# Attention and a mixture of experts in one kernel: an expert's last second layer put between the chains of its tiles

## The chip, the cores and the metric

The kernel runs on one core of a Trainium2 chip. Five engines work from queues of their own: PE (TensorE, matmuls and transposes), DVE (VectorE), ACT (ScalarE), POOL (GpSimd) and SP, which here only starts transfers. They wait for each other by semaphores. The metric is the device time in microseconds; below 0.2% of it, about 1 us, two kernels can't be told apart here.

## The reference, cut to what matters

```python
scores = scale * np.matmul(q, k.transpose(0, 1, 3, 2))     # 4 x 8 heads, 576 x 64, fp32
scores = np.where(block_i >= block_j, scores, -1000000000.0)
attn_out = np.matmul(softmax(scores), v)
x = attn_out.transpose(0, 2, 1, 3).reshape(2304, 512)
logits = x @ w_gate                                        # 8 experts
expert_idx = np.argmax(logits, axis=1)
# each token goes to one expert, the first 576 tokens of an expert are kept
h = np.maximum(np.einsum('ecd,edf->ecf', disp, w1), 0.0)   # 512 -> 1024
y = np.einsum('ecf,efd->ecd', h, w2)                       # 1024 -> 512
out[i] = gate_w[i] * y[expert_idx[i], pos[i]]
```

How many tokens each expert gets is known only while the kernel runs.

## The kernel before, in words

Until about 231 us the kernel computes the attention, writes its rows to DRAM and sorts tokens into lists, one list for each expert. The change leaves this part alone but for three small operations. The rest is the expert stage.

**Slots and tiles.** The expert stage walks through nine slots, z = 0 to 8. Slot 0 is expert 0 with the tokens that were known early, slot 1 the rest of expert 0, and slots 2 to 8 are the other experts that have tokens at all. A slot has 1 to 5 tiles of 128 tokens. In this run the slots 0 to 6 have 3, 3, 1, 1, 5, 1 and 4 tiles, 18 in all, and slots 7 and 8 are empty.

**A tile.** `xin` transposes the tile's x on PE (4 transposes), ACT casts the result to `xh`, and DVE subtracts to get the rest `xl`. `l1(z, t, f)` is one half of the first layer: 12 matmuls of 128x512, each product being three (high by high, high by low, low by high), followed by ACT's relu into `hr[f]`. `htr` transposes `hr` on PE, ACT casts `hh`, and DVE subtracts `hl`. `l2` is the second layer, 24 matmuls in all, and `l2_out` scales the result on DVE (`yo`) and scatters it from POOL. `hh` and `hl` stand in one buffer each, so that the second layer of one tile must be through before the next tile's `htr` ends.

**Software pipeline.** `chain(z, t)` runs the first layer of tile t, then the second layer of the tile *before* it, then the transposes of h of tile t. For t = 0 the tile before is the last tile of the slot before, whichever that was. At t = 0 the chain also prepares the x of the next slot's first tile, `xin(z + 1, 0)`.

**Chains and branches.** `more(z, t, cnt)` puts each further tile into an `If` that is nested in the one before. `rest(z)` puts each further slot into an `If` with an `Else` that holds the last second layer. Every engine takes its own branch. Where the remaining tiles aren't there, each engine runs a short block that waits until it has finished its own work, raises its semaphores by what the skipped tiles would have raised, and jumps to the join. Work after the join can wait only for these raised counts. The counts of tiles are loaded into registers of all engines (`cnt`, L911), before slot 1.

**Weights.** Each expert's weights are 8 chunks of 512 KB, which pass through a ring of 8 buffers in the order of `STREAM`. `prep` of a chunk is an ACT cast to `whi`, a DVE subtraction to `wlo`, and the start of the load that comes next in the ring. `splits(z)` merges 8 of them evenly with the units of `chain(z, 0)`.

Of the kernel before, what the change touches and what calls it, by code (L numbers as in the profile page):

```python
# [39 lines left out]
FIRST_TILE = "RRRFRRRRFRRRFRHRHHR"  # L40
# [11 lines left out]
def attn_moe_kernel(  # L52
# [11 lines left out]
    nc = tc.nc  # L64
# [115 lines left out]
    on_i = const.tile([1, NZ, CT - 1], I32, name="on_i")  # L180
    idf = const.tile([P, E, FR, 2], F32, name="idf")
# [10 lines left out]
    def init_consts():  # L192
# [8 lines left out]
        nc.gpsimd.tensor_scalar_add(eid, iota8[0:1], float(E))  # L201
        nc.vector.tensor_tensor(
# [200 lines left out]
    def c_counts():  # L403
# [25 lines left out]
        has_more(ctl[:, 0, :], 1, NZ)  # L429

# [319 lines left out]
    HC = KF // 4 * 2  # L750
# [64 lines left out]
    def second(ws):  # L815
        return [lambda f=f: l2(ws, f, f + KF // 4) for f in range(0, KF, KF // 4)] + [l2_out]
# [8 lines left out]
    def first(z, t):  # L825
        us = [lambda: l1(z, t, 0), lambda: l1(z, t, 1), lambda: xin(z, t + 1)]
# [30 lines left out]
    def splits(z):  # L857
        if z == 1:
            return preps(G0, G0 + KD)
        g = G0 + KD + NCH * (z - 2)  # L860
        return preps(g, g + NCH)

    def tile_units(z, t):
# [3 lines left out]
    def chain(z, t, cnt):  # L867
# [92 lines left out]
```

## Time and profile before

| | |
|---|---|
| device time, median of 3 runs | 509.03 us (508.82 to 509.41) |
| the profiled execution, its own time | 505.01 us |
| its span in the trace | 503.3 us |
| PE busy | 456.6 us, 91% of the span |
| DVE, ACT, POOL busy | 278.0, 261.0, 117.9 us |
| mean granted PE clock | 0.977 of full speed |

The profiled execution is 1.71 us longer than its span, and 4.02 us shorter than the median of the timed runs. In the rows further down a number in square brackets is the time for which an engine stood idle just before, with what released it. L881 is the line of `more`'s `If`, so that a release by "ACTq L881" comes from ACT's branch block and not from an arithmetic instruction.

### The profile page before, as it was taken

How to read it: one execution, taken by the hardware profiler on the slowest of the kernel's cores; microseconds unless marked ns; L12 is line 12 of the kernel's file. 1: busy time of each engine (PE TensorE's matmuls, PEld its weight loads, DVE VectorE, ACT ScalarE, POOL GpSimd, SP SyncE). 2: the span in 40 equal slices, each digit the busy share in tenths (PEclk: the TensorE clock that was granted, in tenths of full speed). 3: DMA queues.
4: the chain of work that ended last, by engine and by line, in shares of the span. 5: the costliest groups of instructions: out<-in, count | busy, mean ns of one | idle time of the engine just before them, and what ended most of it. 6: DMA issues, size and time to landing. Idle time of an engine off the chain costs nothing. (4 is left out here: it accounts for less than half of the span.)

```text
span 503.3 us, 8359 instructions
## 1 busy us (share of the span) xinstructions
PE 456.6 (91%) x2786; PEld 365.1 (73%) x2786; DVE 278.0 (55%) x566; ACT 261.0 (52%) x613; POOL 117.9 (23%) x166
## 2 busy tenths in 40 slices
PE   5999999999999999989896999688999999899961
PEld 4777777777777777866675778566888888678851
DVE  7666677965696777944722332287662226772210
ACT  4877777777865976762222332268542217652200
POOL 6000001241113200131341411314242114252110
PEclk9999999999999999999999999889899999999977
DMA  4633656668463331112275320077991004992000
GB/s 113 147 77 72 188 145 192 157 125 232 142 192 92 84 70 46 43 34 78 83 224 210 117 85 22 21 264 238 315 317 55 22 21 152 307 308 102 21 29 17
DMA packets 87964, 64.90 MB, mean 129 GB/s; under 512 B 69866, under 2 KB 69866, under 8 KB 87904
## 3 DMA queue, kind: packets, MB, share of 16 engines
q1 hardware_dynamic: 83392, 55.26, 37.5%
q0 software_dynamic: 4512, 8.89, 5.4%
q8 instruction: 31, 0.51, 0.4%
q14 instruction: 29, 0.24, 0.2%
HBM read 53.54 MB, written 14.22 MB: 135 GB/s over the span
## 5 line engine op out<-in xcount | busy, mean ns | idle before, releaser
L589 ACT ACTIVATE p<-s,nm 128x512 f32<-128x512 f32 (+5 forms) x126 | 62.7, 501 | 36.7 <-DVE nm L588 33.1
L780 PE MATMUL h<-whi,xh 128*128 128x512 f32 x144 | 59.7, 415 | 11.9 <-ACTq L881 6.4
L784 ACT ACTIVATE hr<-h 128x512 f32<-128x512 f32 x36 | 21.5, 598 | 85.4 <-PE h L780 76.7
L588 DVE TENSOR_REDUCE nm<-s 128x1 f32<-128x512 f32 (+5 forms) x126 | 54.5, 450 | 19.3 <-PE s L582 14.0
L582 PE MATMUL s<-kh,bdh 128*128 128x192 f32 (+6 forms) x158 | 56.9, 360 | 5.9 <-ACT p L589 3.5
L803 PE MATMUL y<-whi,hh 128*128 128x512 f32 x144 | 58.6, 407 | 4.0 <-issue 4.0
L780 PE MATMUL h<-whi,xl 128*128 128x512 f32 x144 | 58.2, 404 | 0.0
L780 PE MATMUL h<-wlo,xh 128*128 128x512 f32 x144 | 58.1, 403 | 0.0
L803 PE MATMUL y<-whi,hl 128*128 128x512 f32 x144 | 57.2, 397 | 0.0
L803 PE MATMUL y<-wlo,hh 128*128 128x512 f32 x144 | 57.0, 396 | 0.0
L615 PE MATMUL w<-ident,p 128*128 128x128 f32 x400 | 54.7, 274 | 0.7 <-DVE bdl L547 0.6
L792 ACT CAST hh<-t 128x512 fp32r<-128x512 f32 x36 | 20.2, 594 | 59.3 <-issue 36.8
L641 PE MATMUL xB<-pt,vn 128*64 128x320 f32 (+2 forms) x320 | 49.2, 384 | 1.5 <-ACT pt L625 1.5
L582 PE MATMUL s<-kl,bdh 128*128 128x192 f32 (+6 forms) x158 | 50.0, 316 | 0.0
L582 PE MATMUL s<-kh,bdl 128*128 128x192 f32 (+6 forms) x158 | 49.6, 314 | 0.0
L809 DVE TENSOR_SCALAR yo<-y,itl 128x512 f32<-128x512 f32 x18 | 13.5, 749 | 64.3 <-PE y L803 60.0
L246 POOL DMA_INDIRECT xt<-x_rows,it x32 | 40.3, 1260 | 30.9 <-issue 10.4
L615 PEld LDWEIGHTS w<-ident,p 128*128 128x128 f32 x400 | 44.1, 141 | 4.7 <-issue 3.6
L149 POOL TENSOR_TENSOR wlo<-stg,whi 128x1024 fp32r<-128x1024 f32 x8 | 19.0, 2370 | 114.9 <-ACT whi L148 114.9
L149 DVE TENSOR_TENSOR wlo<-ring,whi 128x1024 fp32r<-128x1024 f32 x29 | 35.0, 1220 | 19.3 <-ACT whi L148 19.3
L769 DVE TENSOR_TENSOR xl<-t,xh 128x512 fp32r<-128x512 f32 x25 | 16.8, 688 | 50.7 <-ACT xh L768 50.7
L780 PEld LDWEIGHTS h<-whi,xh 128*128 128x128 f32 x144 | 28.2, 196 | 19.6 <-ACTq L881 7.1
(162 smaller groups left out, 861.2 us busy)
## 6 DMA issues: line engine op xcount, KB each, us to landing
ring<-in_moe_w_dram SPq DMA_DIRECT2D x34, 512.0 KB
stg<-in_moe_w_dram SPq DMA_DIRECT2D x26, 512.0 KB
out_dram<-xt SPq DMA_DIRECT2D x6, 768.0 KB
vn<-in_v_dram SPq DMA_DIRECT2D x32, 128.0 KB
x_rows<-xr SPq DMA_DIRECT2D x16, 256.0 KB
qn<-in_q_dram SPq DMA_DIRECT2D x30, 128.0 KB
kn<-in_k_dram SPq DMA_DIRECT2D x30, 128.0 KB
qn<-in_q_dram SPq DMA_DIRECT2D x16, 32.0 KB
```

Source lines behind the costliest of these rows:

```text
L149: tc.keep_in_program_order((nc.gpsimd if s == 0 else nc.vector).tensor_sub(lo, t, hi.bitcast(F32)))
L246: nc.gpsimd.indirect_dma_start(out=xt(z, t)[0:r], out_offset=None, in_=xd[0:rows], in_offset=bass.IndirectOffsetOnAxis(ap=it[z % NIT][0:r, ...
L582: nc.tensor.matmul(ps[:, 0:w], qs[i][:, b].rearrange("p j q -> p (j q)"), ks[:, a:a + w], start=(x == 0), stop=(x == 2),)
L588: nc.vector.tensor_reduce(nm[:, b:b + 1], pss[0][:, 0:n], axis=AX.X, op=ALU.max, negate=True)
L589: nc.scalar.activation(p_sb[i][b][:, 0:n], pss[0][:, 0:n], AF.Exp, bias=nm[:, b:b + 1], accum_out=sums[bi % 2][:, b % 2, hp, b // 2:b // 2 ...
L615: nc.tensor.transpose(ps[:, o:o + P], p_sb[i][b][:, t * P:(t + 1) * P], ident)
L641: nc.tensor.matmul(xp[j * D:(j + 1) * D, (b0 - r0) * BLK:(b0 - r0 + nb) * BLK], vn[:, t, j, :], pv[:, :, j, :], start=first and n_ == 0, s ...
L769: nc.vector.tensor_sub(xl, pv, xh.bitcast(F32))
L780: nc.tensor.matmul(ps, x_[:, kc], w_[:, fs], start=(kc == 0 and x == 0), stop=(kc == KD - 1 and x == 2))
L784: nc.scalar.activation(hr[f], ps, AF.Relu)
L792: nc.scalar.copy(hh[:, sl], pv)
L803: nc.tensor.matmul(ycur[0], h_[:, fc], w_, start=(fc == 0 and x == 0), stop=(fc == KF - 1 and x == 2))
```

## The change

The last second layer of a slot leaves `chain(z + 1, 0)` and stands in a function of its own, `tail(z)`, behind the join of the slot's branches and ahead of the next slot's branch; `rest` needs no `Else` then. `htr` and `l2` go by three pieces of h, (0,4), (4,6) and (6,8). For t of 1 and more they alternate: a piece of `l2` of the tile before, then the transposes of the same piece. For t = 0, with no second layer inside, the order is `l1`, `l1`, first piece of `htr`, `xin(z, 1)`, `xin(z + 1, 0)`, second and third piece. The eight splits part into four of the first layer, among the first six units of `chain(z, 0)`, and four of the second layer, in `tail(z)`. Each slot's count is loaded at the end of its `chain(z, 0)` instead of eight in a row, and `slot_i` tells PE ahead of time which way a slot's branch will go. PSUM is dealt out anew: `ps_h` 3 to 2 banks, `ps_y` 2 to 1, `ps_t` 3 to 5. Both gathers of slot 0 are issued before its first tile, and the first tile's units are interleaved with the routing in another order.

```diff
-FIRST_TILE = "RRRFRRRRFRRRFRHRHHR"
+FIRST_TILE = "RRRTTRRRRTRRRTRRTTTTR"
...
-    STREAM += [(1, c) for c in range(KD)]
-    for s in range(1, E):
-        if s + 1 < E:
-            STREAM += [(s + 1, c) for c in range(KD)]
-        STREAM += [(s, c) for c in range(KD, NCH)]
+    STREAM += [(s, c) for s in range(1, E) for c in range(NCH)]
...
-    ps_h = ctx.enter_context(tc.tile_pool(name="ps_h", bufs=3, space=PSUM))
-    ps_y = ctx.enter_context(tc.tile_pool(name="ps_y", bufs=2, space=PSUM))
-    ps_t = ctx.enter_context(tc.tile_pool(name="ps_t", bufs=3, space=PSUM))
+    ps_h = ctx.enter_context(tc.tile_pool(name="ps_h", bufs=2, space=PSUM))
+    ps_y = ctx.enter_context(tc.tile_pool(name="ps_y", bufs=1, space=PSUM))
+    ps_t = ctx.enter_context(tc.tile_pool(name="ps_t", bufs=5, space=PSUM))
...
+    PIECES = [(0, 4), (4, 6), (6, 8)]
...
-    def htr(f):
+    def htr(f0, f1):
         ps = ps_t.tile([P, 512], F32, tag="t", name="t")
-        pv = ps.rearrange("p (k n) -> p k n", n=P)
-        for x in range(4):
-            nc.tensor.transpose(pv[:, x, :], hr[f][:, x * P:(x + 1) * P], ident)
-        sl = slice(4 * f, 4 * f + 4)
-        nc.scalar.copy(hh[:, sl], pv)
-        nc.vector.tensor_sub(hl[:, sl], pv, hh[:, sl].bitcast(F32))
+        pv = ps.rearrange("p (k n) -> p k n", n=P)[:, 0:f1 - f0]
+        for fc in range(f0, f1):
+            nc.tensor.transpose(pv[:, fc - f0, :], hr[fc // 4][:, fc % 4 * P:(fc % 4 + 1) * P], ident)
+        nc.scalar.copy(hh[:, f0:f1], pv)
+        nc.vector.tensor_sub(hl[:, f0:f1], pv, hh[:, f0:f1].bitcast(F32))
...
+    def tile_units(z, t):
+        us = [lambda: l1(z, t, 0)]
+        if t + 1 < CT:
+            us.append(lambda: tell(z, t))
+        us += [lambda: l1(z, t, 1), lambda: xin(z, t + 1)]
         if t == 0:
+            us.insert(-1, lambda: htr(*PIECES[0]))
             us.append(lambda: xin(z + 1, 0))
-        return us
-
-    def turn(z, t):
-        return [lambda: keep_ids(z, t), lambda: htr(0), lambda: htr(1)]
+        for x, f in enumerate(PIECES):
+            if t:
+                us.append(lambda f=f: l2(ws_of(z), *f))
+            if t and x == len(PIECES) - 1:
+                us.append(l2_out)
+            if t or x:
+                us.append(lambda f=f: htr(*f))
+        return us + [lambda: keep_ids(z, t)]
...
-        if t + 1 < CT:
-            tell(z, t)
-        if t + 2 < CT:
+        if t + 2 < CT and (z, t) != (0, 1):
             gather(z, t + 2, ROWS0 if z == 0 else N)
         if t == 0:
             fetch(z)
-        for u in merge(tile_units(z, t), splits(z) if t == 0 else []):
+        us = tile_units(z, t)
+        for u in merge(us[:6], splits(z, 0)) + us[6:] if t == 0 else us:
             u()
-        more(z, t + 1, cnt)
+        more(z, t + 1, cnt if t else count(z))
+
+
+    def tail(z):
+        tc.no_sync_barrier()
+        if 0 < z < NZ - 1:
+            on = nc.values_load(
+                slot_i[0:1, z:z + 1], engines=[mybir.EngineType.PE], min_val=0, max_val=1,
+                skip_runtime_bounds_check_because="a comparison")
+            tc.mark_branch_hint_location(f"slot{z}", hint=on, engines=[mybir.EngineType.PE])
+        for u in merge(second(ws_of(z)), splits(z, 1)):
+            u()
...
     def rest(z):
-        if z == NZ:
-            for u in second(ws_of(z - 1)):
-                u()
-            return
-        with tc.If(cnt[z - 1] > 0, preferred_fallthrough_block=True) as some:
-            chain(z, 0, cnt[z - 1])
-            rest(z + 1)
-        with some.Else():
-            for u in second(ws_of(z - 1)):
-                u()
+        if z < NZ:
+            with tc.If(active > z - 1, preferred_fallthrough_block=True, label=f"slot{z - 1}"):
+                chain(z, 0)
+                tail(z)
+                rest(z + 1)
```

How the instructions stand now is shown at three places. Here is PE at the end of slot 1 in the kernel before: the branch block of the skipped tiles (L881, the block waits for PE's own count), the register loads, the branch of `rest`, and the first layer of slot 2.

```order
L881 UNCONDITIONAL_BRANCH
L881 UNCONDITIONAL_BRANCH [waits PE_49]
L881 UNCONDITIONAL_BRANCH [waits PE_49,PE_sequencer_49] x3
L911 TENSOR_LOAD ctl_i x7
L925 COMPARE_AND_BRANCH
L835 TENSOR_LOAD on_i
L956 BRANCH_PREFETCH_HINT
L780 MATMUL h<-whi_3111,xh_3127 128x512 [waits Activation_49]
L780 MATMUL h<-wlo_3112,xh_3127 128x512
L780 MATMUL h<-whi_3111,xl_3128 128x512 [waits DVE_49]
```

The first matmul behind the join waits for the count that ACT raises in its branch block, and the third one for DVE's.

The same place of the changed kernel, on PE, down to the end of the tail's second layer (L807 is the matmul of `l2`, L947 the branch of `rest`, L785 the matmul of `l1`).

```order
L903 UNCONDITIONAL_BRANCH
L903 UNCONDITIONAL_BRANCH [waits PE_49]
L903 UNCONDITIONAL_BRANCH [waits PE_49,PE_sequencer_49] x3
L934 TENSOR_LOAD slot_i
L894 TENSOR_LOAD slot_i
L976 BRANCH_PREFETCH_HINT
L807 MATMUL y<-whi_72,hh 128x512 [waits DVE_49,Activation_49]
L807 MATMUL y<-wlo_73,hh 128x512
L807 MATMUL y<-whi_72,hl 128x512
```

The first matmul behind the join is now one of `l2`, and it waits for the counts of both ACT and DVE; seven register loads have left, two have come. At the end of the same tail stands:

```order
L807 MATMUL y<-whi_78,hl 128x512 [waits DVE_49]
L807 MATMUL y<-whi_78,hh 128x512
L807 MATMUL y<-wlo_79,hh 128x512
L807 MATMUL y<-whi_78,hl 128x512
L947 COMPARE_AND_BRANCH
L785 MATMUL h<-whi_3114,xh_3130 128x512
L785 MATMUL h<-wlo_3115,xh_3130 128x512
L785 MATMUL h<-whi_3114,xl_3131 128x512
```

The next slot's first layer follows the tail with no wait of its own.

The third place is DVE in the first tile of slot 2. Before, from behind the join (`wlo` are the splits, `yo` and `hl` the work of `l2_out` and `htr`):

```order
L149 TENSOR_TENSOR wlo_65<-ring_3371,whi_64 128x1024
L149 TENSOR_TENSOR wlo_67<-stg_61,whi_66 128x1024
L769 TENSOR_TENSOR xl_3132<-t,xh_3131 128x512
L769 TENSOR_TENSOR xl_3130<-t,xh_3129 128x512
L149 TENSOR_TENSOR wlo_69<-stg_62,whi_68 128x1024
L149 TENSOR_TENSOR wlo_71<-stg_63,whi_70 128x1024
L149 TENSOR_TENSOR wlo_3120<-ring_3367,whi_3119 128x1024
L149 TENSOR_TENSOR wlo_3122<-ring_3368,whi_3121 128x1024
L809 TENSOR_SCALAR yo<-y,itl 128x512
L149 TENSOR_TENSOR wlo_3124<-ring_3369,whi_3123 128x1024
L793 TENSOR_TENSOR hl<-t,hh 128x512
L149 TENSOR_TENSOR wlo_3126<-ring_3370,whi_3125 128x1024
```

The changed kernel, a slot's first tile on DVE, down to its branch (L144 the splits, L797 `hl`, L774 `xl`, the first of them for the slot's own next tile and the second for the next slot):

```order
L144 TENSOR_TENSOR wlo_3115<-ring_3380,whi_3114 128x1024
L144 TENSOR_TENSOR wlo_3117<-ring_3381,whi_3116 128x1024
L797 TENSOR_TENSOR hl<-t,hh 128x512
L144 TENSOR_TENSOR wlo_3119<-ring_3382,whi_3118 128x1024
L774 TENSOR_TENSOR xl_3135<-t,xh_3134 128x512
L144 TENSOR_TENSOR wlo_3121<-ring_3383,whi_3120 128x1024
L774 TENSOR_TENSOR xl_3131<-t,xh_3130 128x512
L797 TENSOR_TENSOR hl<-t,hh 128x256 x2
L876 TENSOR_LOAD ctl_i
L903 COMPARE_AND_BRANCH
```

Four of the eight `wlo` stand in this chain now, and the last two pieces of `hl` stand behind all of them. The first `xl` has two `wlo` ahead of it as before, and a third one with a piece of `hl`.

## Rows read from the trace of the kernel before

**Rows 1.** The page, part 1: busy time, share of the span, instructions.

```profile
PE 456.6 (91%) x2786; PEld 365.1 (73%) x2786; DVE 278.0 (55%) x566; ACT 261.0 (52%) x613; POOL 117.9 (23%) x166
```

**Rows 2.** Waits of PE, 235 to 504 us: total, times, longest.

```profile
PE h L780 <- ACTq L881: 6.4, 3, 2.1
...
PE t L767 <- DMA xt<-x_rows,it: 3.6, 2, 3.0
...
PE h L780 <- ACT hh L792: 0.9, 1, 0.9
```

**Rows 3.** Timeline of PE, five stretches: start, length, work [idle before <-releaser].

```profile
275.30 0.63 PE L767 MATMUL t<-ident,xt 128*128 128x128 f32 x4 [1.71 <-DVEq L881]
...
288.94 0.66 PE L790 MATMUL t<-ident,hr 128*128 128x128 f32 x4 [0.64 <-DVE xl L769]
...
290.00 0.49 PE L780 MATMUL h<-whi,xh 128*128 128x512 f32 x1 [0.41 <-ACT xh L768]
...
318.99 0.49 PE L780 MATMUL h<-whi,xh 128*128 128x512 f32 x1 [4.21 <-PEq L835]
...
326.16 0.60 PE L767 MATMUL t<-ident,xt 128*128 128x128 f32 x4
...
415.26 0.47 PE L780 MATMUL h<-whi,xh 128*128 128x512 f32 x1
...
420.81 1.03 PE L767 MATMUL t<-ident,xt 128*128 128x128 f32 x8
...
421.61 0.48 PE L803 MATMUL y<-whi,hh 128*128 128x512 f32 x1
...
427.17 1.04 PE L790 MATMUL t<-ident,hr 128*128 128x128 f32 x8
...
430.33 0.50 PE L780 MATMUL h<-whi,xh 128*128 128x512 f32 x1 [2.13 <-ACTq L881]
...
484.93 0.77 PE L803 MATMUL y<-whi,hh 128*128 128x512 f32 x1 [4.01 <-issue]
...
492.67 0.39 PE L803 MATMUL y<-whi,hl 128*128 128x512 f32 x1
```

**Rows 4.** Busy time by windows; the third number from the end is the granted clock.

```profile
320.00:322.00 2.00, 2.00 (x6) 1.55 (x5) 0.00 (x0) 0.00 (x0) 0.00 (x0) 0.50 0.00 0
...
354.00:356.00 2.00, 2.00 (x6) 1.52 (x6) 1.80 (x3) 0.00 (x0) 1.23 (x2) 0.50 0.99 376
...
428.00:434.00 6.00, 3.87 (x18) 3.02 (x17) 5.73 (x7) 2.75 (x6) 2.10 (x2) 1.00 0.94 339
```

**Rows 5.** Timeline of ACT, the first tile of the expert at 415 us.

```profile
418.35 0.60 ACT L784 ACTIVATE hr<-h 128x512 f32<-128x512 f32 x1 [2.12 <-PE h L780]
...
425.36 2.96 ACT L148 CAST whi<-ring 128x1024 fp32r<-128x1024 f32 x3
...
429.63 0.61 ACT L792 CAST hh<-t 128x512 fp32r<-128x512 f32 x1
```

**Rows 6.** Timeline of DVE, the same tile.

```profile
419.92 1.23 DVE L149 TENSOR_TENSOR wlo<-ring,whi 128x1024 fp32r<-128x1024 f32 x1 [2.86 <-ACT whi L148]
...
427.25 2.35 DVE L149 TENSOR_TENSOR wlo<-ring,whi 128x1024 fp32r<-128x1024 f32 x2
```

**Rows 7.** Groups by shape: busy time, mean ns of one.

```profile
L793 DVE TENSOR_TENSOR hl<-t,hh 128x512 fp32r<-128x512 f32 x36 | 23.7, 686 | 3.1 <-ACT hh L792 2.8 <-issue 0.3
...
L792 ACT CAST hh<-t 128x512 fp32r<-128x512 f32 x36 | 20.2, 594 | 59.3 <-issue 36.8 <-PE t L790 22.6
...
L622 ACT COPY pt<-w 128x256 f32<-128x256 f32 x15 | 5.3, 357 | 0.1
...
L627 DVE COPY pt<-w 128x256 f32<-128x256 f32 x1 | 0.4, 425 | 1.9 <-ACT pt L625 1.9
```

**Rows 8.** Sequencer instructions of two lines: ns min/median/max, first and last start.

```profile
L911 PEldq TENSOR_LOAD <-ctl_i x8: 295/307/468, 288.9 to 318.0; - x8
...
L881 POOLq INC_SWDGE_SEM  x6: 796/1068/1520, 277.6 to 485.5; - x6
```

More of the change, by code (lines that the diff above doesn't have):

```diff
@@ L180, in attn_moe_kernel @@
     on_i = const.tile([1, NZ, CT - 1], I32, name="on_i")
+    ranks = const.tile([1, E], F32, name="ranks")
+    slot_i = const.tile([1, E + 1], I32, name="slot_i")
     idf = const.tile([P, E, FR, 2], F32, name="idf")
@@ L201, in init_consts @@
         nc.gpsimd.tensor_scalar_add(eid, iota8[0:1], float(E))
+        nc.gpsimd.tensor_scalar_add(ranks, iota8[0:1], float(E) + 0.5)
         nc.vector.tensor_tensor(
@@ L429, in c_counts @@
         has_more(ctl[:, 0, :], 1, NZ)
+        act = sm_p.tile([1, E + 1], F32, tag="act", name="act", bufs=1)
+        nc.vector.tensor_reduce(act[:, E:E + 1], nz, axis=AX.X, op=ALU.add)
+        nc.vector.tensor_tensor(
+            act[:, 0:E], act[:, E:E + 1].to_broadcast([1, E]), ranks, op=ALU.is_gt)
+        nc.vector.tensor_copy(slot_i, act)
     def c_units(b, order):
@@ L749, in attn_moe_kernel @@
     hl = mst.tile([P, KF, P], F32R, name="hl")
-    HC = KF // 4 * 2
+    PIECES = [(0, 4), (4, 6), (6, 8)]
     def x_of(z, t):
@@ L815, in second @@
     def second(ws):
-        return [lambda f=f: l2(ws, f, f + KF // 4) for f in range(0, KF, KF // 4)] + [l2_out]
+        return [lambda f=f: l2(ws, *f) for f in PIECES] + [l2_out]
     def keep_ids(z, t):
@@ L822, in keep_ids @@
         nc.gpsimd.tensor_copy(itl[:, 0:1], ids[:, t, 0:1])
-    def first(z, t):
-        us = [lambda: l1(z, t, 0), lambda: l1(z, t, 1), lambda: xin(z, t + 1)]
+    def tile_units(z, t):
[3 more added lines that the diff above has]
+        us += [lambda: l1(z, t, 1), lambda: xin(z, t + 1)]
         if t == 0:
+            us.insert(-1, lambda: htr(*PIECES[0]))
             us.append(lambda: xin(z + 1, 0))
-        return us
-    def turn(z, t):
-        return [lambda: keep_ids(z, t), lambda: htr(0), lambda: htr(1)]
+        for x, f in enumerate(PIECES):
[6 more added lines that the diff above has]
+        return us + [lambda: keep_ids(z, t)]
     def tell(z, t):
@@ L855, in fetch, with splits, count, chain @@
             gather(z + 1, 1)
[L857 to L863, printed above, removed]
-        us = second(ws_of(z) if t else ws_of(z - 1))
-        return us + first(z, t) + turn(z, t) if (z, t) == (1, 0) else first(z, t) + us + turn(z, t)
-    def chain(z, t, cnt):
-        if t + 1 < CT:
-            tell(z, t)
-        if t + 2 < CT:
+    def splits(z, layer):
+        g = G0 + NCH * (z - 1) + KD * layer
+        return preps(g, g + KD) if z else []
+    def count(z):
+        return nc.values_load(
+            ctl_i[0:1, 0, z - 1:z], min_val=0, max_val=CT, skip_runtime_bounds_check_because=why) if z else m0
+    def chain(z, t, cnt=None):
+        if t + 2 < CT and (z, t) != (0, 1):
             gather(z, t + 2, ROWS0 if z == 0 else N)
@@ L885, in attn_moe_kernel @@
     m0 = nc.values_load(m0_i, min_val=0, max_val=CT, skip_runtime_bounds_check_because=why)
-    gather(0, 2, ROWS0)
+    for t in range(2, min(4, CT)):
+        gather(0, t, ROWS0)
     xin(0, 0)
-    tell(0, 0)
-    units = {"F": first(0, 0)[:3], "H": turn(0, 0), "R": c_units(B - 1, ROUTE_LAST) + [c_counts]}
+    us = tile_units(0, 0)
+    del us[5]
+    units = {"T": us, "R": c_units(B - 1, ROUTE_LAST) + [c_counts]}
     for u in FIRST_TILE:
@@ L909, in attn_moe_kernel @@
     more(0, 1, m0)
-    cnt = [
-        nc.values_load(ctl_i[0:1, 0, s:s + 1], min_val=0, max_val=CT, skip_runtime_bounds_check_because=why)
-        for s in range(E)
-    ]
+    active = nc.values_load(
+        slot_i[0:1, E:E + 1], min_val=1, max_val=E, skip_runtime_bounds_check_because="a count of experts")
     orders(NS + 2, E)
     xin(1, 0)
-    chain(1, 0, cnt[0])
+    for u in second(ws_of(0)):
+        u()
+    chain(1, 0)
+    tail(1)
     def rest(z):
-        if z == NZ:
-            for u in second(ws_of(z - 1)):
-                u()
-            return
-        with tc.If(cnt[z - 1] > 0, preferred_fallthrough_block=True) as some:
-            chain(z, 0, cnt[z - 1])
-            rest(z + 1)
-        with some.Else():
-            for u in second(ws_of(z - 1)):
-                u()
+        if z < NZ:
[3 more added lines that the diff above has]
+                rest(z + 1)
     rest(2)
```

## The prediction

> **What bounds the kernel now.** The page's first part says that PE is busy for 91% of the span and DVE and ACT for about half [rows 1], so I read PE's timeline and ask only where it stands still or runs slowly. The view of PE's waits over the expert stage names few causes; the largest is "ACTq L881", 6.4 us in three waits [rows 2]. L881 is the `If` between tiles, so PE waits there for another engine's branch block: the short block that first drains that engine and then raises its counts. The timeline puts every large gap at a place where a slot ends: 1.71 us behind slot 0, 4.21 behind slot 1, 2.13 behind slots 2, 3 and 5, 4.01 behind slot 6 [rows 2, 3].
>
> A gap costs twice. [...] A first layer lasts 5.55 us at full clock (415.26 to 420.81) and 7.17 after the 4.21 gap (318.99 to 326.16): 1.62 lost. A second layer lasts 5.56 (421.61 to 427.17); after the 4.01 gap its 24 starts take 484.93 to 492.67 plus one interval of 0.23, that is 7.97: 2.41 lost [rows 3].
>
> **The single-tile slots (2, 3 and 5), the largest term.** Today the second layer of the slot before and all of PE's transposes follow the first layer without a gap; from one first layer to the next the slot at 415.26 takes 15.07 us (to 430.33) [rows 3]. After the change PE has only the first layer and four groups of four transposes (eight take 0.80, from 420.81 to 421.61), and is through at T + 5.55 + 1.6 = T + 7.2, T being the start of the first layer. Then it meets the join, and its next matmul waits for the counts that ACT and DVE raise in their blocks, that is, for all that they have queued.
>
> The engine that drains last is DVE. Its durations are in the rows: `wlo` 1.22, two of them in 2.35, so one each 1.13 (0.09 overlaps); `hl` 0.69, and `xl`, of the same shape, alike, so one each 0.60 [rows 6, 7]. The half-size `hl` isn't in the trace; a 128x256 copy takes 0.425, so one each 0.33 [rows 7]. The bounds would be half and all of 0.69. The order of DVE in the changed chain then runs: first `wlo` at T+4.66 as now [rows 6], second T+5.8. The next is `hl` of the first piece, which needs `hh`: the relu of the first half starts at T+3.09 [rows 5], that of the second 2.8 later at T+5.9, and with 0.5 for it and 0.6 for `hh` that gives T+7.0. ACT's third `whi` takes 0.95 ((2.96 - 1.06) / 2, [rows 5]), so `wlo` starts at T+7.9, `xl` T+9.0, the fourth `wlo` T+9.7, the other `xl` T+10.8, `hl` T+11.4 and T+11.8, done at T+12.2. From the last cast's end on ACT (429.63 + 0.61) to PE's start at 430.33 a release takes 0.09 [rows 3, 5], which rounding hides. PE idles 5.0 us, runs the tail's 24 matmuls in 5.5 and reaches the next slot at T+17.7. Against 15.07 that is +2.6 for each, **+7.9** for three.
>
> The gap of 5.0 is longer than the 4.21 and 4.01 which lowered the clock, so I let it fall each time, at the mean of the two prices, 2.0: **+6.0**. The next first layer follows the tail with no gap, so what slots 3 and 4 lose now at their start goes away; by the price of 1.62 that is **-3.2**.
>
> **First to second tile (slots 1, 4, 6).** The second tile's first layer now follows directly on the transposes. Its third matmul needs `xl` of its own x, which by the count above ends at T+9.7, while PE would be there at T+7.7. That is 2.0 each. Slot 1 already pays 0.64 and 0.41 there [rows 3], slots 4 and 6 nothing: 6.0 - 1.05 = **+5.0**.
>
> **Later tiles (11 of them).** Alternating pieces of `l2` and `htr` add two changes between transposes and matmuls. I price a change at one place of a transpose, 0.80 / 8 = 0.1 [rows 3], an estimate between 0 and 0.2: **+2.2**. The casts of pieces lie behind the next piece's matmuls.
>
> **Slot 4's end.** With five tiles no branch lies ahead of its tail. There is one bank for y, so the tail waits for `yo`, an operation of the size of `hl`: **+0.7**.
>
> **The ends of slots 0, 1 and 6.** Seven register loads of 0.307 [rows 8] leave slot 1's end, which is its excess over 2.13; and no PE branch without a hint stands ahead of the last second layer. What stays at each end is the last piece's cast and subtraction. The 1.71 gap is such a chain with full-size pieces, released by DVE; with 0.36 for 0.59 on ACT and 0.425 for 0.69 on DVE [rows 7] it becomes 1.2. So 1.71 + 4.21 + 4.01 = 9.93 becomes 3.6, **-6.3**, and with gaps of that size I expect the full clock, which gives back 1.62 and 2.41, **-4.0**.
>
> [...] The 4.01 gap ends in "issue": PE waited for nothing that the view knows [rows 3], behind a branch, 2.8 us longer than the 1.2 above. [...]
>
> **The rest.** Both gathers of slot 0 are issued ahead of its first tile, and slot 6's has more time with longer chains: the waits for `xt`, **-3.6** [rows 2], with 0 as the other bound. In slot 0's first tile `htr` starts earlier, which takes away the wait for `hh`, **-0.9** [rows 2], bounds -0.9 and 0; three small DVE operations added to the counts lie under PE's matmuls there, and would push this toward 0. At the program's end POOL has one more block of skipped work to raise counts for, 1.07 [rows 8], ahead of its last drain: **+1.1**, bounds 0 and 2.1. The four splits in the tail take ACT 3.9 and DVE 4.5 us beside 5.5 of PE: nothing, and if they ran over they would meet the next `wlo` only 4.7 us on. Loads of weights come in another order, with 2.6 us more per single-tile slot; at a DMA share of 0.99 in the busiest window [rows 4] that is relief, so nothing.
>
> **Sum.** 7.9 + 6.0 - 3.2 + 5.0 + 2.2 + 0.7 - 6.3 - 4.0 - 3.6 - 0.9 + 1.1 = +4.9. Against the profiled execution's 505.01 this is 509.9; that execution is 4.0 below the median of the runs shown, so the forecast is 509.03 + 4.9 = **513.9**. With the bounds above (clock 1.62 or 2.41 each, changes 0 or 0.2, the waits for `xt` kept) the likeliest case alone reaches from 510.5 to 518.
>
> **Rivals.**
> *B, the clock falls at the short gaps too.* The 2.0 us in front of second tiles are as long as the gaps of 2.13, of which the one ahead of the window at 354 lowered the clock and the one inside the window from 428 did not [rows 4]. Three falls at 1.62 add 4.9: 518.8. Against it: the two matmuls in the midst of the wait.
> *D, the clock does not fall at the tails.* Nothing in the rows speaks for it but the 2.13 gap with clock 1.00 [rows 4]. Without the 6.0: 507.9, no change or just faster.
> *C, the other side: the tail starts on its first piece.* If the tail's first matmul needed only the first `hh` and `hl`, done at T+7.6, and the release came at T+8.2 with PE through its sequencer's loads, each tail would start 4.0 earlier and the clock stay: 513.9 - 12.0 - 6.0 = 495.9. It decides from T+10.6 on, where three times 1.6 us eats the 4.9. Against it stands that the matmul behind the join waits for both blocks' counts, and that the 1.71 gap was ended by DVE's block [rows 3].
> [...]
>
> **Chances.** Forecast 0.60, B 0.14, D 0.14, C 0.08, E 0.04. A measurement tells 0.2%, 1.0 us, from no change. Faster: C, half of D and a little of the forecast's low side, 0.17. Same: 0.10 from D and the forecast's edge. Slower: 0.73. The range leaves out C, E, the low side of D and the high side of B, together about 0.19: 506.5 to 520.5.
>
> **What would show it.** In the changed profile PE should stand about 5 us ahead of the second layer's first matmul behind slots 2, 3 and 5, released by DVE's branch block, with the clock at 0.50 just after; a wait of 2 us for `xl` in front of three second tiles; about 1.2 us behind slots 0, 1 and 6; 17.7 us plus the clock's loss from one single-tile slot to the next; no wait for `xt`. The prediction is wrong if the tails' gaps are under 3.5 us, because DVE drains sooner than by this count, or if gaps of 1.2 us or "issue" stand where I have them otherwise.

## The result, and the profile after

| | before | after |
|---|---|---|
| median, 4 runs each | 509.22 us (508.82 to 509.58) | 517.08 us (515.18 to 517.87) |
| profiled execution, its span | 505.01, 503.3 us | 517.61, 515.8 us |
| PE busy | 456.6 us (91%) | 460.9 us (89%) |

The ratio is 1.0149, with a 95% interval of 1.0119 to 1.0180: slower by 1.5%, 7.9 us, where 4.9 were forecast. The two profiles lie 12.6 us apart, since the profiled execution of before was a short one; that is taken up below.

The waits of PE in the expert stage, after (total, times, longest), answer to [rows 2]:

```profile
PE y L807 <- DVEq L903: 15.7, 4, 4.8
PE h L785 <- ACT xh L773: 2.7, 3, 0.9
PE h L785 <- DVE xl L774: 1.9, 3, 0.6
PE y L807 <- PEq L894: 1.7, 1, 1.7
PE t L772 <- DVEq L903: 1.1, 1, 1.1
PE y L807 <- DVE yo L813: 0.8, 1, 0.8
```

L903 is the `If` between tiles, L807 the matmul of `l2`, L785 that of `l1`. DVE's block has taken the place of ACT's: three waits of 4.83 and one of 1.16. Behind slot 1 PE's own sequencer still releases it, at its load of `slot_i` (L894): 1.70 in place of 4.21, and not the 1.2 of the forecast. No wait for `xt` is left.

PE's timeline, after, against [rows 3]:

```profile
285.93 0.50 PE L785 MATMUL h<-whi,xh 128*128 128x512 f32 x1 [0.91 <-ACT xh L773]
...
287.30 0.50 PE L785 MATMUL h<-whi,xl 128*128 128x512 f32 x1 [0.64 <-DVE xl L774]
...
294.04 0.60 PE L772 MATMUL t<-ident,xt 128*128 128x128 f32 x4
...
320.69 0.39 PE L785 MATMUL h<-whi,xh 128*128 128x512 f32 x1
...
332.88 0.77 PE L807 MATMUL y<-whi,hh 128*128 128x512 f32 x1 [4.83 <-DVEq L903]
...
339.90 0.39 PE L785 MATMUL h<-whi,xh 128*128 128x512 f32 x1
...
359.70 0.39 PE L785 MATMUL h<-whi,xh 128*128 128x512 f32 x1
...
426.02 0.39 PE L785 MATMUL h<-whi,xh 128*128 128x512 f32 x1
...
445.33 0.39 PE L785 MATMUL h<-whi,xh 128*128 128x512 f32 x1
...
494.63 0.47 PE L807 MATMUL y<-whi,hh 128*128 128x512 f32 x1 [1.16 <-DVEq L903]
...
499.96 0.39 PE L807 MATMUL y<-whi,hl 128*128 128x512 f32 x1
```

320.69 is the start of slot 2, and PE's tail of that slot begins at 332.88, 12.19 us later (12.2 was forecast). The next first layers stand at 339.90, 359.70 and, for slot 5, 426.02 and 445.33: 19.21, 19.80 and 19.31 us for a single-tile slot, in place of 15.07 plus at times 1.6. In slot 1 the third matmul of the second tile waits for `xl`, as forecast, and starts at T + 9.63 (T is 277.67 there; 9.7 was forecast). The larger part of the wait, 0.91, stands ahead of the first matmul, for `xh` from ACT, which the forecast did not have. From the third matmul on 22 matmuls take 6.74 us (287.30 to 294.04), 0.306 each. That was not in the likeliest case.

The windows, after (the third number from the end is the granted clock), against [rows 4]:

```profile
288.00:290.00 2.00, 2.00 (x7) 1.56 (x6) 1.64 (x4) 0.00 (x0) 0.00 (x0) 0.57 0.86 234
...
333.00:335.00 2.00, 2.00 (x5) 1.62 (x6) 2.00 (x2) 1.95 (x3) 0.00 (x0) 0.50 0.86 313
353.00:355.00 2.00, 2.00 (x6) 1.54 (x5) 2.00 (x3) 1.09 (x2) 0.00 (x0) 0.50 0.97 334
439.00:441.00 2.00, 2.00 (x6) 1.60 (x5) 2.00 (x3) 1.21 (x2) 0.00 (x0) 0.50 0.98 364
494.60:500.00 5.40, 5.37 (x24) 4.42 (x24) 3.50 (x3) 3.73 (x4) 2.10 (x3) 1.00 0.49 162
```

The clock stands at 0.57 behind the second tile's wait, at 0.50 in the windows of all three tails, and at 1.00 in the tail of slot 6, which the wait of 1.16 precedes.

DVE's timeline in slot 2, after, the order that the third place of the change shows, with times:

```profile
325.24 2.36 DVE L144 TENSOR_TENSOR wlo<-ring,whi 128x1024 fp32r<-128x1024 f32 x2 [2.40 <-ACT whi L143]
327.52 0.68 DVE L797 TENSOR_TENSOR hl<-t,hh 128x512 fp32r<-128x512 f32 x1
328.45 1.23 DVE L144 TENSOR_TENSOR wlo<-ring,whi 128x1024 fp32r<-128x1024 f32 x1 [0.25 <-ACT whi L143]
329.59 0.69 DVE L774 TENSOR_TENSOR xl<-t,xh 128x512 fp32r<-128x512 f32 x1
330.19 1.22 DVE L144 TENSOR_TENSOR wlo<-ring,whi 128x1024 fp32r<-128x1024 f32 x1
331.33 0.69 DVE L774 TENSOR_TENSOR xl<-t,xh 128x512 fp32r<-128x512 f32 x1
331.93 0.75 DVE L797 TENSOR_TENSOR hl<-t,hh 128x256 fp32r<-128x256 f32 x2
```

From the first `wlo` on DVE hardly stands idle; the last `hl` ends at 332.68, and PE starts 0.20 later. At T + 11.99 this is the count of the prediction, 12.2, almost to the operation.

At the end, the last scatter (timeline of POOL) and the instruction of POOL's block that raises the counts of the skipped slots (sequencer instructions of the branch of `rest`: ns min/median/max, first and last start), before:

```profile
494.78 0.99 POOL L810 DMA_INDIRECT out_dram<-yo,itl  x1 [9.57 <-POOLq L925]
...
L925 POOLq INC_SWDGE_SEM  x1: 1570/1570/1570, 494.9 to 494.9; - x1
```

The same after, with PE's branches of `rest` (L947):

```profile
501.99 1.19 POOL L814 DMA_INDIRECT out_dram<-yo,itl  x1 [4.09 <-DVE yo L813]
...
L947 POOLq INC_SWDGE_SEM  x1: 1565/1565/1565, 507.4 to 507.4; - x1
...
L947 PEldq COMPARE_BRANCH  x7: 65/65/5028, 316.6 to 502.5; - x7
```

Before, the instruction stands 0.1 us behind the scatter's start; after, at 507.4, it stands 5.4 us behind the start and 4.2 us after the scatter left POOL. It is as long as before. PE's branch of 5.03 us starts at 497.1: it is the jump out of the last slot, which lies under the last second layer now and stood ahead of it before. From PE's last matmul (499.96 + 0.39) to the span's end it takes 15.4 us; it took 10.2 before (492.67 + 0.39 to 503.3).

### The profile page after: what moved, and what is told of

Same layout as the page of the kernel before. It is cut to its first block, busy times and chain, and to the rows that moved or that the text cites. A ratio compares the mean times of both kernels' runs of the same rounds, so it can differ in the third digit from the quotient of the medians.

```text
span 515.8 us, 8436 instructions
## 1 busy us (share of the span) xinstructions
PE 460.9 (89%) x2786; PEld 366.2 (71%) x2786; DVE 285.7 (55%) x591; ACT 268.5 (52%) x635; POOL 118.8 (23%) x167
## 5 line engine op out<-in xcount | busy, mean ns | idle before, releaser
L807 PE MATMUL y<-whi,hh 128*128 128x512 f32 x144 | 62.3, 433 | 18.1 <-DVEq L903 15.7
L785 PE MATMUL h<-whi,xh 128*128 128x512 f32 x144 | 59.4, 412 | 3.3 <-ACT xh L773 2.7
L785 PE MATMUL h<-whi,xl 128*128 128x512 f32 x144 | 58.5, 406 | 1.9 <-DVE xl L774 1.9
L807 PE MATMUL y<-wlo,hh 128*128 128x512 f32 x144 | 58.4, 405 | 0.0
L807 PE MATMUL y<-whi,hl 128*128 128x512 f32 x144 | 58.3, 405 | 0.0
L785 PE MATMUL h<-wlo,xh 128*128 128x512 f32 x144 | 58.0, 403 | 0.0
L814 POOL DMA_INDIRECT out_dram<-yo,itl x18 | 19.6, 1091 | 145.8 <-DVE yo L813 76.1
L796 ACT CAST hh<-t 128x256 fp32r<-128x256 f32 (+1 forms) x54 | 23.5, 452 | 53.8 <-PE t L795 38.5
L797 DVE TENSOR_TENSOR hl<-t,hh 128x256 fp32r<-128x256 f32 (+1 forms) x54 | 27.0, 509 | 40.8 <-ACT hh L796 40.8
L774 DVE TENSOR_TENSOR xl<-t,xh 128x512 fp32r<-128x512 f32 x25 | 17.2, 689 | 56.2 <-ACT xh L773 53.8
L144 DVE TENSOR_TENSOR wlo<-ring,whi 128x1024 fp32r<-128x1024 f32 x30 | 36.2, 1223 | 20.4 <-ACT whi L143 19.8
L807 PEld LDWEIGHTS y<-whi,hh 128*128 128x128 f32 x144 | 28.4, 197 | 24.6 <-ACT whi L143 15.1
L144 POOL TENSOR_TENSOR wlo<-stg,whi 128x1024 fp32r<-128x1024 f32 x8 | 19.0, 2371 | 114.6 <-ACT whi L143 114.6
```

Of the source, the lines that this page charges most:

```text
L144: tc.keep_in_program_order((nc.gpsimd if s == 0 else nc.vector).tensor_sub(lo, t, hi.bitcast(F32)))
L785: nc.tensor.matmul(ps, x_[:, kc], w_[:, fs], start=(kc == 0 and x == 0), stop=(kc == KD - 1 and x == 2))
L796: nc.scalar.copy(hh[:, f0:f1], pv)
L797: nc.vector.tensor_sub(hl[:, f0:f1], pv, hh[:, f0:f1].bitcast(F32))
L807: nc.tensor.matmul(ycur[0], h_[:, fc], w_, start=(fc == 0 and x == 0), stop=(fc == KF - 1 and x == 2))
L814: nc.gpsimd.indirect_dma_start(out=out, out_offset=bass.IndirectOffsetOnAxis(ap=itl[:, 1:2].bitcast(U32), axis=0), in_=y, in_offset=None, ...
```

## The experiments

Twelve runs follow, in the order in which they were made: first four, then four, then three and one; a first form of the last one gave no result. The kernels of each group ran on one chip, with the kernel before beside them.

**The changed kernel again**, as a control for the next three.

> The changed kernel once more, as a control on the same chip as the next three. Both theories: 517 us within 2, a last second layer that ends about 15.4 us ahead of the span's end, 24 matmuls of a tail in 7.2 to 7.8 us behind slots 2, 3 and 5, and a first layer of the second tiles of slots 1, 4 and 6 in which 22 matmuls take 6.9 us.

Measured: 515.03 us against 506.11 of the kernel before on this chip, ratio 1.0184 (1.0136 to 1.0232). The tails' second layers take 7.29, 7.97 and 7.32 us; the second tiles of slots 4 and 6 are slow again (22 matmuls to the end of the last, 6.92 us), that of slot 1 is not (5.27). So the fall of the clock at the tails repeats, and that at second tiles comes and goes.

**The tail's loads later.** The third argument of `preps` says whether a split starts the next load of its ring buffer.

```diff
-        return preps(g, g + KD) if z else []
+        return preps(g, g + KD, layer == 0) if z else []
...
         if t == 0:
+            for x in range(KD if z > 1 else 0):
+                load_after(G0 + NCH * (z - 2) + KD + x)
             fetch(z)
```

> The tail's four splits no longer start the next loads; these loads are issued at the beginning of the next slot's first chain, so that none is issued behind slot 6. Theory: the last scatter of rows shares the queue's engines with four loads of 512 KB that nobody will use, and lands about 5 us late; without them the time from the last matmul to the end of the span falls from 15.4 to about 10.3 us (it was 10.2 before the change), and the whole to about 512. Rival: the longer end is the price of one more skipped slot's block on POOL and of its branch; then the end stays at 15 us and the time at 517.

Measured: 514.51 us, ratio to before 1.0173 (1.0123 to 1.0224), against 515.03 of the control: no change that the runs can tell. In its trace the end is 12.95 us (498.65 to 511.6), half way. The timeline of POOL and the instruction of its block:

```profile
500.30 1.19 POOL L818 DMA_INDIRECT out_dram<-yo,itl  x1 [4.08 <-DVE yo L817]
...
L953 POOLq INC_SWDGE_SEM  x1: 1565/1565/1565, 503.2 to 503.2; - x1
```

The windows in which the scatter starts, in the changed kernel and in this run (the number before the last is the DMA share):

```profile
502.00:504.00 2.00, 0.00 (x0) 0.00 (x0) 0.33 (x1) 0.00 (x0) 1.18 (x1) 0.83 0.83 237
...
500.00:502.00 2.00, 0.00 (x0) 0.00 (x0) 0.63 (x1) 0.00 (x0) 1.19 (x1) 0.71 0.02 8
```

The block now follows the scatter's end (501.49) by 1.7 us instead of 4.2, and the DMA engines, busy with loads in the changed kernel, are nearly idle. So the loads cost 2.5 us by delaying the scatter's landing. The remaining 2.7 are the block's wait for a landing without loads, not its instruction, which is as long in the kernel before: both theories hold in part. That the block waits for the landing is inferred from these times; an earlier scatter of the changed kernel lets POOL go on 1.8 us after it left (495.89 to 497.67). The median cannot show the 2.5 us: between the two traces these and 3.3 less at the second tiles stand against 2.2 more in the tails and 3.1 more ahead of slot 0's second tile.

**The second tile's x ahead of the third split.**

```diff
-        for u in merge(us[:6], splits(z, 0)) + us[6:] if t == 0 else us:
+        if t == 0:
+            ss = splits(z, 0)
+            us = us[:1] + ss[:1] + us[1:2] + ss[1:2] + us[2:5] + ss[2:3] + us[5:6] + ss[3:] + us[6:]
+        for u in us:
```

> In a slot's first chain the third split stands behind the xl of the slot's own second tile instead of ahead of it; all else as in the changed kernel. Theory: the third matmul of the second tile's first layer waits under 0.7 us in place of 0.9 and 0.64, the clock stays at 1.00 there, and its 22 matmuls take 5.2 in place of 6.9; three times 1 + 1.7 gives -8, about 509. Rival: these 22 matmuls are slow because DVE, ACT and the DMAs read and write the same memory at that time; then only the wait goes, -3, about 514. Both: the tails' wait of 4.8 us stays.

Measured: 509.39 us, 5.6 below the control; ratio to before 1.0059 (1.0031 to 1.0088). PE's timeline at slot 1's second tile, and the window behind it:

```profile
284.82 0.40 PE L785 MATMUL h<-wlo,xh 128*128 128x512 f32 x1
285.32 0.50 PE L785 MATMUL h<-whi,xl 128*128 128x512 f32 x1
```

```profile
286.00:288.00 2.00, 2.00 (x11) 1.64 (x10) 2.00 (x3) 1.37 (x4) 0.59 (x1) 1.00 1.07 406
```

Nothing is listed as a wait there; the third matmul starts 0.50 after the second, and the clock stays at 1.00 at a DMA share of 1.07 and with DVE busy throughout. All three second tiles take 6.12 us for 24 matmuls. The rival, contention, is out. Three waits shorter by 1.3 and two falls at 1.6 (as many as the control has) make 7.1; the medians show 5.6, with the control's runs spread over 2.6.

**PE kept busy in the tails' waits.** 14 matmuls that nobody reads, into a bank that is taken from the five of the transposes:

```diff
+        if z in (2, 3, 5):
+            for x in range(14):
+                nc.tensor.matmul(
+                    dum, x_of(z, 0)[0][:, x % KD], w1_of(ws_of(z), x % KD)[0][:, 0:512], start=True, stop=True)
```

> Behind slots 2, 3 and 5 the tail begins with 14 matmuls of 128x512 into a PSUM bank that nobody reads, on operands that have long been there, so that PE works through most of the 4.8 us of its wait. The result is computed as before and 42 matmuls come on top. Theory: the tail's second layer is slow because of the clock, which falls in the wait; with PE busy it stays at 1.00, the 24 matmuls take 5.7 us in place of 7.2 to 7.8, and the time falls by 5, to about 512, though PE has more work. Rival: the splits on ACT and DVE, which run at the same time, slow the matmuls; then the second layers stay at 7.2 us or more and the time at 517.

Measured: 521.09 us (515.49 to 523.22), slower; ratio to before 1.026 (1.019 to 1.0331). As a time the expectation missed; in the trace the theory on the clock holds. PE's timeline, one window, and the branches of the `If`:

```profile
339.31 5.70 PE L902 MATMUL dum<-whi,xh 128*128 128x512 f32 x14 [6.66 <-PEq L896]
...
359.48 3.48 PE L902 MATMUL dum<-whi,xh 128*128 128x512 f32 x14 [1.17 <-PEq L896]
...
362.80 0.39 PE L809 MATMUL y<-whi,hh 128*128 128x512 f32 x1
```

```profile
363.00:368.00 5.00, 5.00 (x23) 4.13 (x22) 3.00 (x3) 1.51 (x2) 0.00 (x0) 1.00 0.99 343
```

```profile
L909 PEldq COMPARE_BRANCH  x21: 65/92/5849, 247.9 to 499.2; - x21
```

Where the added matmuls filled the wait (slots 3 and 5) the tail's second layer takes 5.60 us at a clock of 1.00, with the splits running beside it on ACT and DVE as always. So it is the clock, not the splits, that costs 1.5 to 2.1 us there. Behind slot 2 a branch of PE took 5.85 us, which takes 0.44 at that place in the changed kernel, and the wait became 6.66. Why this branch took so long, no run shows. Of the 9.5 us between the profiled executions of this run and the control, 6.3 lie in slot 2, 4.0 ahead of the expert stage, for which no cause was found, and 4.1 in slot 0: 0.9 in its first tile (14.44 us from the attention's last matmuls to the second tile, 13.52 in the control, and 14.4 in the three later runs that also have four banks for the transposes), 1.6 of clock, and a wait of 2.68 us behind it, ended by "issue", in place of 1.12. Slots 3, 5 and 6 give back 5.0.

**Two splits in the chain, six in the tail.**

```diff
-        return preps(g, g + KD) if z else []
+        return (preps(g, g + 2) if layer == 0 else preps(g - 2, g + KD)) if z else []
```

> Two of a slot's splits stand in its first chain and six in its tail, in place of four and four; all else as in the changed kernel. Theory: DVE's queue sets when a tail may start; two wlo less, 1.13 us each, shorten PE's wait behind slots 2, 3 and 5 from 4.83 to about 2.5 us, and xl of the second tile comes as early as in the run xl_early, so that the time falls by 3 x 2.3 for the tails and 5.5 for the second tiles, from 515 to about 502; where the clock stays up at the shorter waits, 5 less. Rival: the six splits in the tail are in the way there, of the next slot's first layer (its weights) and of yo; then PE waits behind the tail for what it no longer waits for ahead of it, and the time stays above 508.

Measured: 507.36 us, ratio to before 1.0003 (0.9977 to 1.0029), where the unaltered change stands at 1.015 to 1.018 on other chips. The direction is the theory's, the size fell short by 5. DVE's timeline in slot 2 and a row of PE's waits:

```profile
324.63 0.68 DVE L774 TENSOR_TENSOR xl<-t,xh 128x512 fp32r<-128x512 f32 x1
325.45 1.23 DVE L144 TENSOR_TENSOR wlo<-ring,whi 128x1024 fp32r<-128x1024 f32 x1
```

```profile
PE y L807 <- DVEq L903: 11.9, 4, 3.6
```

The merge put the second split behind the first `xl`, where it still delays the drain: the waits are 3.58 and not 2.5, 3.2 in all. And the end takes 18.3 us (487.46 to 505.8), 2.9 more: the block follows the scatter 2.2 us later than in the changed kernel, with six loads started in the tail and not four, and the scatter itself starts 0.7 later (2.38 behind PE's last matmul, 1.64 in the changed kernel), which I put down to `yo`, standing on DVE behind the tail's `wlo`. Those two make up the shortfall. No wait of PE for weights is listed. So the rival's first part is out, and its part on `yo` is worth 0.7 at the end.

**The tail inside the next slot's branch**, with an Else as before.

```diff
-                chain(z, 0)
-                tail(z)
-                rest(z + 1)
+            tail(z - 1)
+            chain(z, 0)
+            rest(z + 1)
+        with some.Else():
+            for u in second(ws_of(z - 1)):
+                u()
```

> The tail's second layer stands inside the next slot's branch, and once more in an Else, without splits, as in the kernel before; pieces, chains and splits as in the changed kernel. Theory: of the longer end (15.4 us from the last matmul to the end of the span, against 10.2 before) half is the four useless loads and half that POOL's block of skipped slots waits for the last scatter to land; with the scatter in the Else both go, 15.4 becomes 10.3, and the time falls by 5 to about 510. Rival: the end depends on the last slot's branch alone, and stays above 13 us as it did without the loads.

Measured: 518.3 us, ratio to before 1.0233 (1.0182 to 1.0284); no gain at all. The end fell to 10.4 us as expected (505.70 to 516.1), but the last second layer came late. PE's timeline and the branches of `rest`:

```profile
498.38 0.77 PE L807 MATMUL y<-whi,hh 128*128 128x512 f32 x1 [5.55 <-issue]
...
L951 PEldq COMPARE_BRANCH  x7: 65/65/4344, 315.2 to 501.3; - x7
```

PE's jump into the Else takes 4.34 us, the wait is 5.55 in place of 1.16, and the clock falls behind it (7.32 us for 24 matmuls). So the kernel before paid the jump ahead of its last second layer, and the changed kernel, whose jump of 5.03 us lies under that layer, pays POOL's block behind the last scatter instead: 4.4 and 1.6 given for 5.0.

**These two together**, with two banks for y.

```diff
-    ps_y = ctx.enter_context(tc.tile_pool(name="ps_y", bufs=1, space=PSUM))
-    ps_t = ctx.enter_context(tc.tile_pool(name="ps_t", bufs=5, space=PSUM))
+    ps_y = ctx.enter_context(tc.tile_pool(name="ps_y", bufs=2, space=PSUM))
+    ps_t = ctx.enter_context(tc.tile_pool(name="ps_t", bufs=4, space=PSUM))
```

> The two runs above together, with two PSUM banks for y and four for the transposes. Theory: the gains add up, 515 - 13 - 5 - 0.8, about 496, below the kernel before. Rival: second layers between the chains always cost the wait for the drain of DVE, and the time comes out no better than before, 506 or more.

Measured: 507.82 us, ratio 1.0025 (0.9993 to 1.0057): the rival's number, though for the Else's reason. The tails' waits are 2.94, the clock fell behind two of the three (second layers of 8.58, 7.32 and 5.72), the wait for `yo` is gone, and the Else's wait is 5.76 with 8.54 us of second layer behind it.

**The kernel before with early gathers alone.**

```diff
-    gather(0, 2, ROWS0)
+    for t in range(2, min(4, CT)):
+        gather(0, t, ROWS0)
...
-        if t + 2 < CT:
+        if t + 2 < CT and (z, t) != (0, 1):
```

> The kernel before with one part of the change alone: both gathers of slot 0 are issued ahead of its first tile. Theory: PE's wait of 3.0 us for xt in slot 0's third tile goes, and with it 3 us, 0.6%. Rival: the gather then meets the scatters of the last lists on POOL, ahead of the first tile, and the wait moves to there; no change.

Measured: 506.16 us against 507.78, ratio 0.9982 (0.9948 to 1.0016): inconclusive as a time. In the trace no wait for `xt` is left, and from the second tile's first layer to slot 0's end it takes 24.7 us (247.45 to 272.18) in place of 27.9. So the step is right in the trace. As a time the interval leaves out the full 3 us, and 23 of the 25 runs of before in that job spread over 503.9 to 509.5.

**Loads later, tail ahead of the branch, both splits ahead of the first `hl`**, and two banks for y.

```diff
-        return preps(g, g + KD) if z else []
+        return (preps(g, g + 2) if layer == 0 else preps(g - 2, g + KD, False)) if z else []
...
-        for u in merge(us[:6], splits(z, 0)) + us[6:] if t == 0 else us:
+        for u in merge(us[:3], splits(z, 0)) + us[3:] if t == 0 else us:
```

> The tail stays ahead of the branch, as in the changed kernel, but two splits stand in the first chain (both ahead of the first hl) and six in the tail, the tail's loads are issued in the next slot's chain, and y has two PSUM banks. Theory: DVE's queue, the useless loads and the clock are the changed kernel's losses; PE waits 2.4 us behind slots 2, 3 and 5, not at all ahead of second tiles, and the end takes 13 us; from two_splits, 507.4, that is 3 x 1.2 for the tails, 5 for the end and 0.8 for y less: about 498, below the kernel before by 1.8%. Rival: what is saved at the tails comes back as waits for late loads or weights; 505 or more.

Measured: 498.73 us against 507.19, ratio 0.9862 (0.9815 to 0.9908): faster than both kernels. PE's waits (slot ends alone; L909 is the `If`):

```profile
PE y L811 <- DVEq L909: 4.2, 3, 1.6
...
PE y L811 <- issue: 1.8, 1, 1.8
PE y L811 <- DVE hl L801: 1.6, 1, 1.6
```

The single-tile slots wait 1.57 to 1.59 us, the clock fell behind one of the three, and the end takes 14.8 us (481.63 to 496.4), longer than expected: the scatter starts 2.51 us behind PE's last matmul, which I put down to `yo` on DVE as in the run with six splits in the tail, and the block 2.7 behind the scatter's end. One wait of 1.78 in the midst of slot 2's tail has no releaser that the view knows; its cause stays open. How much of the gain over the changed kernel comes from the loads, the splits and the second bank is not separated.

**The next slot's x in the tail as well.**

```diff
-            us.append(lambda: xin(z + 1, 0))
...
+        us = second(ws_of(z))
+        us.insert(1, lambda: xin(z + 1, 0))
```

> As best2, and the x of the next slot's first tile is transposed and split in the tail, behind its first piece of the second layer, in place of the chain. Theory: DVE has one xl less ahead of the branch, 0.6 us, so PE waits 1.8 us behind slots 2, 3 and 5, and the clock falls less often: 2 to 5 below best2. Rival: the tail's transposes wait for PSUM banks or the next slot's first layer for xl, and it is no better than best2.

Measured: 498.42 us, ratio 0.9851 (0.9809 to 0.9894), no better than the run before it. PE's timeline in slot 2:

```profile
327.82 0.47 PE L811 MATMUL y<-whi,hh 128*128 128x512 f32 x1 [1.96 <-issue]
```

The waits behind the single-tile slots are 1.96, not 1.8, and the view ends two of the three by "issue" and one by DVE's `hl` (L801). As all three are equally long, I take DVE's queue to set the start still, which is not shown for those two. The start in slot 2 comes 0.6 us earlier, as expected: 8.97 us after the slot's first matmul (318.85), against 9.58 in the run before. The wait is longer because PE is through earlier, and the gain goes because the transposes, which lay inside the wait, now lengthen the tail: 6.29 us from its first matmul to the next slot, against 5.56 for a tail of the run before at full clock.

**The kernel before again**, one execution.

> The kernel before once more, for its profile. Theory: its executions differ by the clock behind the 2.13 us gaps and by PE's branch ahead of the last second layer; of the four places behind slots 1, 2, 3 and 5 other ones than in the first profile may be slow, and the gap of 4.0 behind slot 6 may be up to 6. Rival: the executions differ in the attention alone, and the expert stage repeats itself.

Measured: 510.19 us. PE's timeline, and the branches of `rest` (L925):

```profile
267.52 1.09 PE L767 MATMUL t<-ident,xt 128*128 128x128 f32 x4 [4.47 <-DMA xt<-x_rows,it]
...
490.06 0.77 PE L803 MATMUL y<-whi,hh 128*128 128x512 f32 x1 [5.78 <-issue]
...
L925 PEldq COMPARE_BRANCH  x7: 65/65/5020, 322.2 to 492.9; - x7
```

The wait for `xt` is 4.47 against 2.97, with the clock down behind it (8.15 us for the second layer, 5.70 in the first profile), and the last jump 5.78 against 4.01. That is 5.7 us between two executions of one kernel, at places that the change removes; the jump's wait is 5.42 in the run with early gathers.

**Two pieces of h in place of three**, one execution; `FIRST_TILE` has one unit less.

```diff
-    PIECES = [(0, 4), (4, 6), (6, 8)]
+    PIECES = [(0, 4), (4, 8)]
```

> The changed kernel with h transposed in two pieces, (0,4) and (4,8), in place of three (the first tile's order has one unit less). Theory: the last piece's cast and subtraction are longer by 0.5, so PE's wait behind slot 0 goes from 1.12 to 1.6 us and behind slot 6 from 1.16 to 1.6, while a later tile of a slot, 12.36 us with three pieces, loses one change between transposes and matmuls, 0.05 to 0.1; the tails' waits of 4.83 us stay. Rival: the register loads and branches set these ends, and they stay at 1.1.

Measured: 511.46 us, one run, beside one execution of the kernel before at 500.22; two single runs carry no verdict. PE's waits:

```profile
PE y L807 <- DVEq L903: 17.5, 5, 4.8
...
PE t L772 <- DVEq L903: 1.5, 1, 1.5
```

Behind slots 0 and 6 PE waits 1.55 and 1.59: the third piece is worth 0.43 at an end. A later tile takes 12.37 us, as with three: the second change of kind costs nothing.

## Why the prediction was right, and where its sizes were off

The time lies in the range, and the case in the profiled execution is the forecast's with rival B on top. Against the traces, term by term (they lie 12.6 us apart, of which this table holds 11.8):

| term | forecast | in the trace | from |
|---|---|---|---|
| single-tile slots, full clock | +7.9 | +8.0 | 19.21 + 19.80 + 19.31 less the clock's 5.1, less 3 x 15.07 |
| clock in the tails | +6.0 | +5.1 | second layers of 7.18, 7.79, 7.30 against 5.72 |
| clock no longer lost behind slots 2 and 3 | -3.2 | -3.3 | 16.68 and 16.72 from slot to slot before, less 2 x 15.07; first layers at full clock now |
| waits ahead of second tiles | +5.0 | +3.6 | 3 x 1.55 less 1.05 |
| clock behind these waits | 0 (rival B +4.9) | +4.9 | 22 matmuls 6.90 against 5.27 (slot 1 of the control), three times |
| pieces in later tiles | +2.2 | +1.3 | 12.36 against 12.24, 11 tiles |
| `yo` behind slot 4 | +0.7 | +0.8 | its wait |
| ends of slots 0, 1, 6 | -6.3 | -5.9 | 1.12 + 1.70 + 1.16 against 9.93 |
| their clock | -4.0 | -4.0 | 5.72 behind slots 1 and 6 |
| waits for `xt` | -3.6 | -3.6 | none left |
| first tile, `hh` | -0.9 | -0.3 | second tile's start 245.33 against 245.67 |
| end of the program | +1.1 | +5.2 | 15.4 against 10.2 |

**The tails: right in mechanism and size.** The wait is DVE's queue, counted to 0.2 us; fewer splits ahead of the drain shorten it (4.83, 3.58, 2.94 and 1.58 in four kernels). That the slow second layers come from the clock, which falls in these waits, is shown by the matmuls that kept it up (second layers of 5.60 us at a clock of 1.00).

**The second tiles: the wait right, its consequence underrated.** `xl` came when the count said, and PE waits 1.55 in place of 2.0. I gave rival B 0.14, because two matmuls stand in the midst of the wait. They don't keep the clock (0.57 in the window from 288). But it doesn't always fall: in the five profiles that have this wait of 0.91 and 0.64, it fell in 6 of 15 places, and in the control alone in 2 of 3. As a mean over these executions the term is some 2 us, not 4.9, an estimate from 6 in 15.

**The program's end: mis-sized, by 4.1.** The step "one more block of skipped work, 1.07" priced the block's instruction and not what the block waits for. The instruction is no longer than before (1.57 in both), but where it stood 0.1 us behind the start of the last scatter, it stands 5.4 behind it now: by these times it waits for that scatter to land, and the landing was late by four loads of weights for a slot that is empty. 2.5 us are the loads, 2.7 the wait without them.

**The offset to the median: it did not carry over, and here is luck.** I took the profiled execution as 4.0 below the median in both kernels. The second profile of before shows that its executions differ in the wait for `xt`, the clock behind it and the jump into the Else, all of which the change takes away from PE's path. So an execution like the second one gains several us more by the change than the first profile does, which would explain how 12.6 between the profiles is 7.9 between the medians. The forecast's +4.9 was too small by the end and the second tiles' clock, and this offset took a part of that back; how large each term is in the medians is not shown. Had the offset carried over, the 11.8 of the table would have made 520.8, outside the range. The executions of one kernel also differ by more than the 1 us named at the start, 23 of 25 lying between 503.9 and 509.5 in one job, so that a term of 3 us can't be read from one execution. And in the forecast's own bounds the 518 is too low: clock at 2.41, changes at 0.2 and the waits for `xt` kept come to 513.9 + 1.2 + 2.2 + 3.6 = 520.9.

**Rivals C, D and E.** C is out: in slots 2, 3 and 5 no tail starts before DVE has drained. D is out: 18 of 18 tail waits of 4.7 us or more in six profiles lowered the clock (22 matmuls in 6.5 to 7.9 us behind them, against 5.1 at full clock). E, slot ends that stay as long as the 4.01 of before, did not come about, for PE waits 1.1 to 1.7 there, though a jump out of the last slot is slow in each of the eight profiles in which it was read, 1.98 to 5.03 us: ahead of the last second layer in the kernels with an Else, under or behind it in the others, where PE waits for nothing more. The change hides this jump and does not shorten it. In the run with added matmuls another one, of 5.85, lay on PE's path.

## What to carry to other kernels

An engine's branch block is a drain here: work put behind a join waits for everything that the engines whose counts it needs have queued ahead of it (PE 4.83 us in slot 2, until 0.20 us behind DVE's last `hl`), so before moving work there, move other work (here six of eight splits) from ahead of the branch to behind it; with that, with loads that start only once they are needed and with a second bank for y, the same idea was 1.4% faster than the kernel before, not 1.5% slower. Where a wait stands ahead of a long run of matmuls, price the clock behind it as well as the wait (here 1.5 to 2.1 us behind waits of 4.83). And compare two executions of the kernel before, ahead of a prediction, to see which of its losses come in every run.

## What the hardware showed that was not expected

- **The same gap lowers the clock in one execution and not in the next.** The fall is told by the matmuls behind the gap: 22 of them, counted from the last wait, take 6.0 to 8.0 us where it fell and at most 5.3 where it did not. Gaps of 2.13 us at slot ends did so in 5 of 9 places (three profiles of the kernel before, one of them with early gathers), the waits of 0.91 and 0.64 us in 6 of 15, the tails' waits of 1.57 to 1.59 in 1 of 3, of 1.96 in 1 of 3, of 2.94 in 2 of 3 (one of 2.97 for `xt` in the first profile of before did not), and those of 3.58 and more always (21 places, and 10 other gaps of 4.0 us and more in the expert stage).
- **PE's branches cost 0.065 to 0.09 us where they enter a tile or a slot, and up to 5.85 where they leave one.** Behind slots 0 to 6 they took 0.18 to 0.44 in the first profiles of the two kernels, but 2.08 behind slot 3 of the changed one (under DVE's wait; 0.44 behind slots 2 and 5), and 5.85 behind slot 2 in the run with added matmuls. The jump out of the last slot is slow in all eight profiles in which it was read: 3.41 and 5.02 in the kernel before, 5.03 in the changed one, 1.98 at the least.
- **Loads that nobody waits for can lengthen the end:** four of 512 KB put off POOL's block behind the last scatter by 2.5 us.
